# The first batch of an attention and SwiGLU kernel: its loads in one GpSimd queue, its values among its scores, and tile 0's down projection by halves

## The chip, the cores and the metric

One core of a Trainium2 chip runs the whole kernel. The metric is the device time of one execution in microseconds (us); lower is better.

## What is computed

Selective attention over 8 batches of 8 heads (576 positions, head width 64), and a SwiGLU block on its output (4608 tokens, width 512, hidden width 1536):

```python
scores = 0.125 * q @ k.T                       # per batch and head, 576 x 576
cum = cumsum(maximum(s, 0))
scores = where(causal, -1e9, scores + minimum(-(cum[i] - cum[j]), 0))
attn = exp(scores - max); attn = attn / sum(attn)
x = (attn @ v), heads side by side             # 4608 x 512
out = (silu(x @ w_gate) * (x @ w_val)) @ w_out
```

Inputs and output are float32; the kernel multiplies in bfloat16.

## The kernel before, in words

**Heads and half batches.** The 64 heads are counted through (`bh`), eight per batch; four of them are a half batch (`hb`, 0 to 15). k and q of a half batch are loaded as float32 (`load_one`), cast to bfloat16 (`cast_one`), transposed, and laid into one of two sets of buffers `KQ` (`hb % 2`), two heads to a row (`r`). Half batches 0 to 4 are transposed by TensorE (`pe_transpose`) and copied out of PSUM (`pe_out`: k by ScalarE, q by VectorE); half batches from 5 on go through a scratch in DRAM (`scratch`, buffers `ks`, `qs`) and a DMA transpose (`transposes`, into `pk`, `pq`), and VectorE lays them into `KQ` (`split`). The bias of s is carried by extra rows of `KQ` that small DMAs fill from `HL` (`aug`).

**Scores and values.** `score_piece` multiplies one of four pieces of a head's causal scores (four diagonal blocks; 448 + 64; 320 + 192; 64 columns), and ScalarE takes the exponential (L388) into `pt`. GpSimd then zeroes the upper triangles of the diagonal blocks (L391, L396). In batch 0 the pieces go by pairs into two wide PSUM buffers of 1024 columns, so that there are two exponentials a head; later heads have one bank and one exponential for each piece. `av_piece` multiplies with v (`VT`, cast by `cast_v`, L183), `av_out` divides by the row sum (L429, L430), and x is transposed for the block by TensorE (`x_pe`, batches 0 and 1) or through DRAM (`x_out`, `x_in`).

**The SwiGLU block** works on nine tiles of 512 tokens. For each of 12 column groups `ft`: gate product (L626), tanh on ScalarE (`th`, L631), `pp` on VectorE (L633), value product (L641), `ht` on VectorE (L649). Then the down projection: tiles 0 and 1 by `down_plain` (L670), the rest by a seven product scheme (`down_seven`, L711).

**Order.** Each engine's instructions run in the order in which the code writes them. Batch 0 is written out by hand in `first_batch`: all scores, then all values and x. From then on the generator `ffn_items` yields an item after each product, and after item n the loop pumps the attention of later heads (`attn_items`) to a position that grows evenly with n; in tile 0 this starts after item 6. `hook[n]` holds extra work for item n of tile 0, `PREP_AT` the pieces after which TensorE transposes a coming half batch, `side` the loads, casts and scratch work at given pieces, and `later` the `split` copies, of which one is issued at every fourth item and the rest ahead of the next half batch:

```python
if step == 0:
    do_later(NR * 2)
...
for ci in range(4):
    score_piece(kk, ci)
    side(h, step, ci)
```

**Queues.** k, q and v are loaded by DMAs that SP issues, in the order of the code; the weights, which are cast on the way, and stores are issued by GpSimd. Early in batch 0, SP issues s, k and q of half batches 0 and 1, the bias rows, v of batch 0 and k, q of half batch 2; at head 7 it issues k, q 3, v of batch 1, k, q 4 and 5. GpSimd issues gate and value weights at heads 1, 4 and 5, and `wo` at head 7.

**PSUM.** `take` gives out the bank that was released the longest ago, `give` returns it; after batch 0 the two wide buffers and four single ones are replaced by eight single banks.

Of the kernel before, what the change touches and what calls it, by code (L numbers as in the profile page):

```python
# [12 lines left out]
FP32 = mybir.dt.float32  # L13
# [6 lines left out]
def kernel(  # L20
# [86 lines left out]
    PTP = {0: first, "bufs": 8}  # L107

    with tc.manual_schedule():
# [3 lines left out]
        first_psum = ExitStack()  # L113
        psa = first_psum.enter_context(tc.tile_pool(name="psa", bufs=1, space=PSUM))
        bank = {}
        for i in range(2):
            bank["w", i] = psa.tile([128, 1024], FP32, name=f"wide{i}")
        for i in range(4):
            bank["s", i] = psa.tile([128, 512], FP32, name=f"one{i}")
        released = {key: i - 8 for i, key in enumerate(bank)}  # L120
# [3 lines left out]
        def take(kind="s"):  # L124
            b = min((x for x in bank if x[0] == kind), key=lambda x: released[x])
            assert released[b] < OPEN
            released[b] = OPEN
            return b
# [5 lines left out]
        def second_psum():  # L134
            assert all(x < OPEN for x in released.values())
            at_end = dict(released)
            first_psum.close()
            psb = ctx.enter_context(tc.tile_pool(name="psb", bufs=1, space=PSUM))
            bank.clear()
            released.clear()  # L140
            for i in range(8):
                bank["s", i] = psb.tile([128, 512], FP32, name=f"bank{i}")
                released["s", i] = at_end["w", i // 2] if i < 4 else at_end["s", i - 4]

# [6 lines left out]
        def load_one(hb, name, rs=(0, NR)):  # L151
# [3 lines left out]
            nc.sync.dma_start(  # L155
# [10 lines left out]
        def load_v(b, cs):  # L166
# [3 lines left out]
            for c in cs:  # L170
                n = 128 if c < 4 else TAIL
                nc.sync.dma_start(
# [13 lines left out]
        NEGS2 = -1.0058441162109375  # L186

# [22 lines left out]
        load_qk(1)  # L210
# [6 lines left out]
        make_identity(nc, ident)  # L217

# [10 lines left out]
        pads(0)  # L229
        init_vt(0)  # L230
        init_vt(1)
        nc.vector.memset(aug_rows(1, 0), 0.0)
        nc.gpsimd.memset(aug_rows(1, 1), 0.0)
        pads(1)
# [113 lines left out]
        scs = {}  # L348

        def score_piece(bh, ci):  # L350
            hb, hh = divmod(bh, HB)
            pair = bh < H
            if ci == 0:
                pts[bh] = PTP[0].tile(
                [128, PTW], BF16, tag="pt", bufs=PTP["bufs"], name="pt"
            )
# [3 lines left out]
            if pair:  # L360
                if ci % 2 == 0:
                    bs = take("w")
                    scs[bh] = bs
                else:
                    bs = scs[bh]
                base = (512, 0, 0, 512)[ci]
            else:
                bs = take()
                base = 0
            o = base  # L370
            n = sum(hi - lo for _, lo, hi in CHUNKS[ci])
            sc = view(bs, 1024 if pair else 512)
            for (tj, lo, hi) in CHUNKS[ci]:
# [5 lines left out]
                    start=True,  # L379
                    stop=True,  # L380
                )
                o += w
            if not pair or ci % 2 == 1:
                if pair:
                    c0, W = ((576, 1024), (0, 576))[ci // 2]
                else:
                    c0, W = CHUNK_PT[ci], n
                nc.scalar.activation(pt[:, c0 : c0 + W], sc[:, 0:W], AF.Exp, scale=0.125)  # L388
                give(bs)
            if ci == (1 if pair else 0):  # L390
# [90 lines left out]
        def side(h, step, ci):  # L481
            bh = HB * h + step
            if bh == H + 3 and ci == 1:
                for c in range(5):
                    cast_v(1, c, nc.gpsimd)
            if h >= 3 and h + 3 < NHB and (step, ci) == (0, 1):
                load_qk(h + 3)
            hb = h + 1
            if NPE <= hb < NHB:
                late = hb == NPE  # L490
                if (step, ci) == (0, 1):
# [515 lines left out]
```

The softmax here doesn't subtract the row's maximum and nothing guards it: scores larger than these inputs give would overflow.

## Time and profile before

| | |
|---|---|
| Median of 9 runs | 379.78 us (378.94 to 381.06) |
| The profiled execution's own time | 379.78 us |
| Its span in the profile | 378.0 us |
| TensorE busy (matmuls) | 362.9 us |
| VectorE busy | 290.4 us |
| ScalarE busy | 242.6 us |
| GpSimd busy | 207.1 us |
| First matmul at | 5.40 us |
| First gate product at | 31.56 us |

The profile shows one execution. PE is TensorE, PEld its loading of weights, DVE is VectorE, ACT ScalarE, POOL GpSimd and SP SyncE, which only issues DMAs here. A busy TensorE is not one at its peak: four matmuls of 512 columns in a row show 379 ns each, but follow each other every 0.86 us by four. What counts for the end is when TensorE stands still. The span leaves out about 1.8 us around the program that the time contains.

### The profile page before, as it was taken

To read this page: it belongs to the slowest core of one execution; us is meant where nothing else is said; L and a number is where in the kernel's file an instruction comes from. 1 tells how busy PE (TensorE), PEld (TensorE's weight loads), DVE (VectorE), ACT (ScalarE), POOL (GpSimd) and SP (SyncE) were. 2 spreads that over 40 slices of the span, in tenths; PEclk is the share of its full clock that TensorE was granted. 3 is DMA by queue.
4 is the path that set the end of the run, shared out by engine and by line. 5 is a ranking of instruction groups with operands and counts; after the bars stand their busy time and mean duration, and the time that the engine had idled before them with its cause. 6 is when DMAs were issued, how large, how long until landed. Compare 5 with 4: busy or idle time off the path is not lost.

```text
span 378.0 us, 8674 instructions
## 1 busy us (share of the span) xinstructions
PE 362.9 (96%) x3246; PEld 230.3 (61%) x3246; DVE 290.4 (77%) x577; ACT 242.6 (64%) x459; POOL 207.1 (55%) x326
## 2 busy tenths in 40 slices
PE   3879999999999999999999999999999999999996
PEld 3666556655555545865586558655875575466465
DVE  8766787457894899769975998589958876985984
ACT  7686788677976877578766885697365523323321
POOL 7684348545374646595559556875675426224320
PEclk9999999999999999999999999999999999999999
DMA  7999999997477998499769765986223133001103
GB/s 250 186 252 263 198 249 278 343 269 162 166 181 241 220 294 212 111 249 249 197 186 285 199 161 164 237 207 144 51 73 111 25 27 128 0 2 69 42 2 111
DMA packets 100729, 64.22 MB, mean 170 GB/s; under 512 B 81888, under 2 KB 85824, under 8 KB 100688
## 3 DMA queue, kind: packets, MB, share of 16 engines
q1 hardware_dynamic: 91248, 46.15, 49.2%
q0 software_dynamic: 9440, 17.53, 18.4%
q8 instruction: 25, 0.41, 0.4%
q14 instruction: 16, 0.13, 0.1%
HBM read 37.90 MB, written 19.86 MB: 153 GB/s over the span
## 4 chain that ended last, share of the span: by engine, by line
PE 87%; DVE 4%; DMA 3%; ACT 3%; issue 1%; SPq 0%; DVEq 0%; ACTq 0%
PE bank L626 22%; PE bank L641 22%; PE bank L711 17%; PE bank L375 9%; PE bank L413 7%; PE bank L670 5%; DMA pk<-ks 2%; PE wide L375 2%; DVE pp L633 1%; ACT pt L388 1%; DVE kq L326 1%; DMA rawq<-in_q_dram 1%; DVE ht L649 1%; PE one L413 1%; PE one L311 1%
## 5 line engine op out<-in xcount | busy, mean ns | idle before, releaser
L388 ACT ACTIVATE pt<-bank 128x512 bf16<-128x512 f32 x224 | 106.8, 506 | 25.8 <-PE bank L375 17.0
L626 PE MATMUL bank<-XT,wg 128*128 128x512 bf16 x432 | 110.8, 379 | 0.8 <-DVE ht L649 0.3
L641 PE MATMUL bank<-XT,wv 128*128 128x512 bf16 x432 | 110.9, 379 | 0.0
L631 ACT ACTIVATE th<-bank 128x512 bf16<-128x512 f32 x108 | 64.7, 599 | 58.9 <-PE bank L626 54.6
L633 DVE SCALAR_TENSOR_TENSOR pp<-th,bank 128x512 bf16<-128x512 bf16 x108 | 73.7, 683 | 24.3 <-ACT th L631 23.7
L649 DVE SCALAR_TENSOR_TENSOR ht<-pp,bank 128x512 bf16<-128x512 bf16 x108 | 74.1, 687 | 10.4
L658 POOL TENSOR_TENSOR ht<-ht 128x512 bf16<-128x512 bf16 x35 | 40.4, 1155 | 53.0 <-DVE su L656 52.9
L375 PE MATMUL bank<-kq 128*128 128x128 bf16 (+4 forms) x504 | 67.5, 240 | 0.2 <-DVE ht L649 0.2
L375 PEld LDWEIGHTS <-kq 128*128 128x128 bf16 x576 | 47.0, 100 | 32.7 <-issue 5.3
L626 PEld LDWEIGHTS <-wg 128*128 128x128 bf16 x432 | 38.4, 98 | 35.2 <-issue 1.2
L641 PEld LDWEIGHTS <-wv 128*128 128x128 bf16 x432 | 38.3, 98 | 35.3
L391 POOL TENSOR_SCALAR_AFFINE_SELECT pt<-pt 128x512 bf16<-128x512 bf16 x64 | 41.8, 653 | 30.0 <-ACT pt L388 29.3
L413 PEld LDWEIGHTS <-pt 128*128 128x128 bf16 x960 | 41.0, 98 | 16.6 <-issue 0.8
L413 PE MATMUL bank<-vt,pt 128*128 128x65 bf16 x840 | 41.8, 194 | 0.5 <-DVE ot L430 0.5
L447 POOL DMA_DIRECT2D xs<-ot x24 | 21.7, 906 | 28.1 <-DVE ot L430 28.1
L711 PEld LDWEIGHTS <-ht 128*128 128x128 bf16 x336 | 31.2, 98 | 4.3
L197 POOL DMA_DIRECT2D kq<-HL x52 | 32.1, 619 | 0.1
L430 DVE TENSOR_TENSOR ot<-bank,rc 128x320 bf16<-128x320 f32 x56 | 27.5, 491 | 1.9
L396 POOL TENSOR_SCALAR_AFFINE_SELECT pt<-pt 128x64 bf16<-128x64 bf16 x64 | 17.3, 270 | 18.5 <-ACT pt L388 18.4
L711 PEld LDWEIGHTS <-su 128*128 128x128 bf16 x252 | 23.6, 98 | 3.3
L670 PE MATMUL bank<-wo,ht 128*128 128x512 bf16 x96 | 24.6, 379 | 0.0
L776 POOL TENSOR_TENSOR ysb<-ysb 128x512 f32<-128x512 f32 x12 | 15.2, 1270 | 15.3 <-DVE ysb L770 15.3
(96 smaller groups left out, 397.7 us busy)
## 6 DMA issues: line engine op xcount, KB each, us to landing
rawk<-in_k_dram SPq DMA_DIRECT2D x15, 576.0 KB
rawq<-in_q_dram SPq DMA_DIRECT2D x15, 576.0 KB
rawv<-in_v_dram SPq DMA_DIRECT2D x32, 256.0 KB
out_dram<-ysb POOLq DMA_DIRECT2D x32, 256.0 KB, 3.7
xs<-ot POOLq DMA_DIRECT2D x24, 160.0 KB, 3.7
ks<-ck SPq DMA_DIRECT2D x11, 288.0 KB
qs<-cq SPq DMA_DIRECT2D x11, 288.0 KB
wg<-in_moe_w_gate_dram POOLq DMA_DIRECT2D x2, 768.0 KB, 12.9
```

Of the source, the lines that this page charges most:

```text
L375: nc.tensor.matmul(sc[:, o : o + w], T[:, 1, e * S + 128 * tj : e * S + 128 * (tj + 1)], T[:, 0, e * S + lo : e * S + hi], start=True, sto ...
L388: nc.scalar.activation(pt[:, c0 : c0 + W], sc[:, 0:W], AF.Exp, scale=0.125)
L391: nc.gpsimd.affine_select(pt[:, 1088:1600], pt[:, 1088:1600], pattern=[[0, 4], [1, 128]], compare_op=ALU.is_ge, fill=zreg, base=0, channel ...
L413: nc.tensor.matmul(av[:, bi * (D + 1) : (bi + 1) * (D + 1)], pt[:, c0 : c0 + 128], VT[b % 2][:, tj, h, :], start=(tj == 0), stop=(tj == bi),)
L626: nc.tensor.matmul(pg, WG[j][:, c, f0 : f0 + 128], xt[:, c, :], start=(c == 0), stop=(c == 3),)
L631: nc.scalar.activation(th, pg, AF.Tanh, scale=0.5)
L633: nc.vector.scalar_tensor_tensor(pp, in0=th, scalar=1.0, in1=pg, op0=ALU.add, op1=ALU.mult)
L641: nc.tensor.matmul(pv, WV[j][:, c, f0 : f0 + 128], xt[:, c, :], start=(c == 0), stop=(c == 3),)
L649: nc.vector.scalar_tensor_tensor(hp[:, 2 * k2 : 2 * k2 + 2, :].rearrange("p a n -> p (a n)"), in0=pp, scalar=0.5, in1=pv, op0=ALU.mult, op ...
L658: (nc.vector if ft == NFT - 1 else nc.gpsimd).tensor_sub(hp[:, 1:3, :], hp[:, 1:4:2, :], hp[:, 0:3:2, :])
L670: nc.tensor.matmul(py, hps[ft // 2][:, 2 * (ft % 2) + half, c0 : c0 + 128], WO[ft // WKO][:, ft % WKO, :], start=(ft == 0), stop=(ft == NF ...
L711: nc.tensor.matmul(ps, lhs(p), rhs(p), start=(first and p == 0), stop=(last and p == NP - 1), skip_group_check=True,)
```

## The change

In batch 0 the wide buffers go; every piece of scores has a bank and an exponential of its own, and the causal mask is added by a matmul (`ident` with `lower`, a tile of 0 and -32768) instead of GpSimd's selects. Values and the transposes of x are written between the scores of later heads, from head 4 on. Of each of the first three column groups, three of the four gate products of tile 0 are written ahead of the last x (`products`, which keeps a begun bank). k, q 1, v 0, the weights of gate and value (now in halves), k, q 2 to 5, v 1 and v 2 are loaded through GpSimd's queue, in the order in which they are used; all of v 0 is cast on GpSimd. `hook` spreads the later loads over tile 0. k, q 3 are transposed later, and k, q 5 are cast and go through the scratch later. In `prep_one` the second copy out of PSUM is put off to the next item (`seconds`). In tile 0 the down projection does the first half of the hidden width for all four groups of 128 tokens, then the second half, with four banks open.

```diff
-    PTP = {0: first, "bufs": 8}
+    PTP = {0: first, "bufs": 7}
+    lower = first.tile([128, 512], BF16)
...
-            bank["w", i] = psa.tile([128, 1024], FP32, name=f"wide{i}")
...
+        bank = {i: psb.tile([128, 512], FP32, name=f"bank{i}") for i in range(8)}
...
+        nc.gpsimd.memset(lower, 0.0)
+        nc.gpsimd.affine_select(
+            lower, lower, pattern=[[0, 4], [1, 128]],
+            compare_op=ALU.is_ge, fill=nc.gpsimd.to_reg(MASKED), base=0, channel_multiplier=-1,
+        )
...
+        for nm in ("k", "q"):
+            load_one(1, nm, eng=nc.gpsimd)
         init_vt(0)
...
+            masked_here = masked and ci in (0, 3)
+            if masked_here:
+                nc.tensor.matmul(
+                    sc, ident, lower[:, 0:n], start=True, stop=False, skip_group_check=True
+                )
...
+            nc.scalar.activation(pt[:, c0 : c0 + n], sc, AF.Exp, scale=0.125)
+            give(bs)
+            if masked:
+                return
...
         def side(h, step, ci):
             bh = HB * h + step
-            if bh == H + 3 and ci == 1:
+            if bh == H + 4 and ci == 1:
                 for c in range(5):
                     cast_v(1, c, nc.gpsimd)
+            if h == 4 and (step, ci) in ((0, 1), (2, 1)):
+                load_qk(6 + step // 2)
...
+                if late and (step, ci) == (0, 0):
+                    cast_one(hb, "k", nc.scalar)
+                if late and (step, ci) == (0, 2):
+                    cast_one(hb, "q", nc.scalar)
+                if late and (step, ci) == (1, 0):
+                    scratch(hb)
+                if late and (step, ci) == (1, 1):
+                    transposes(hb)
...
-                first = 1 if hb < NPE + 2 else 0
+                first = 2 if late else 1 if hb < NPE + 3 else 0
...
         def prep_one(hb, i):
...
-            for r in range(2):
-                pe_out(hb, nm, g, r, nc.scalar if nm == "k" else nc.vector)
+            eng = nc.scalar if nm == "k" else nc.vector
+            pe_out(hb, nm, g, 0, eng)
+            seconds.append(lambda: pe_out(hb, nm, g, 1, eng))
         PREP_AT = {
-            2: {(0, 3): 0, (1, 3): 1, (2, 1): 2, (2, 3): 3},
+            2: {(2, 0): 0, (2, 2): 1, (3, 0): 2, (3, 2): 3},
...
+        def products(kind, ft, xt, cs=range(4)):
+            j, f0 = divmod(ft * 128, WCH)
+            w = (WG if kind == "g" else WV)[j]
+            if (kind, ft) in begun:
+                bs, c0 = begun.pop((kind, ft))
+                cs = range(c0, 4)
+            else:
+                bs = take()
+            for c in cs:
+                nc.tensor.matmul(
+                    view(bs, TT), w[:, c, f0 : f0 + 128], xt[:, c, :],
+                    start=(c == 0), stop=(c == 3),
+                )
+            if cs[-1] < 3:
+                begun[kind, ft] = bs, cs[-1] + 1
+            return bs
...
         def down_plain(tt, hps):
...
+            order = [(ts_, j) for ts_ in range(4) for j in range(NWCH)]
+            if tt == 0:
+                order.sort(key=lambda x: x[1])
+            for ts_, j in order:
+                yield from part(ts_, j)
...
+        keep_warm(32)
         cast_half(0, "k", 0, nc.scalar)
         cast_half(0, "q", 0, nc.scalar)
         aug(0, SP4)
+        row_half("k", 0, nc.scalar)
+        row_half("q", 0, nc.vector)
+        cast_half(0, "k", 1, nc.scalar)
+        cast_half(0, "q", 1, nc.gpsimd)
+        load_v(0, (0, 1), nc.gpsimd)
+        nc.gpsimd.memset(aug_rows(1, 1), 0.0)
+        pads(1)
+        aug(1, SP4)
+        load_v(0, (2, 3, 4), nc.gpsimd)
+        w_load("g", 0)
+        keep_warm(10)
+        row_half("k", 1, nc.scalar)
+        row_half("q", 1, nc.vector)
+        keep_warm(10)
+        cast_one(1, "k", nc.vector)
+        cast_one(1, "q", nc.vector)
+        for c in range(3):
+            cast_v(0, c, nc.gpsimd)
+        w_load("v", 0, 0)
+        for c in range(3, 5):
+            cast_v(0, c, nc.gpsimd)
+        for nm in ("k", "q"):
+            load_one(2, nm, eng=nc.gpsimd)
+        w_load("v", 0, 1)
+        for nm in ("g", "v"):
+            w_load(nm, 1, 0)
+        for nm in ("k", "q"):
+            load_one(3, nm, eng=nc.gpsimd)
+        for nm in ("g", "v"):
+            w_load(nm, 1, 1)
+        scores(0)
+        half_batch("k")
+        scores(1)
+        half_batch("q")
+        scores(2)
+        scores(3)
...
+        load_v(1, range(5), nc.gpsimd)
+        scores(4)
+        values(0, 1)
+        scores(5)
+        values(2, 3)
+        scores(6)
+        values(4)
+        x_pe(0, nc.vector)
+        scores(7)
+        aug(3, SP4)
+        values(5)
+        x_pe(1, nc.vector)
+        values(6)
+        x_pe(2, nc.scalar)
+        values(7)
+        for ft in range(3):
+            products("g", ft, XT[:, :, 0:TT], range(3))
+            if ft == 0:
+                x_pe(3, nc.scalar)
...
+        for i in range(4):
+            at_item(3 + i, prep_one, 2, i)
+        at_item(8, load_one, 4, "k", (0, NR), nc.gpsimd)
+        at_item(10, cast_one, 3, "k", nc.gpsimd)
+        at_item(11, w_load, "o", 0)
+        at_item(13, w_load, "o", 1)
...
-            n0 = 6 if tt == 0 else 0
+            n0 = 7 if tt == 0 else 0
```

`row_half` transposes and copies one row of half batch 0, `half_batch` transposes k or q of half batch 1 and copies its first row, `scores(h)` is four times `score_piece`, `values` is `av_piece` and `av_out`, and `keep_warm(n)` multiplies `ident` with itself n times into a spare bank.

## The prediction

> **What bounds the kernel now.** I read the page's busy times first:
>
> ```profile
> span 378.0 us, 8674 instructions
> PE 362.9 (96%) x3246; PEld 230.3 (61%) x3246; DVE 290.4 (77%) x577; ACT 242.6 (64%) x459; POOL 207.1 (55%) x326
> ```
>
> TensorE is idle for 378.0 - 362.9 = 15.1 us. By the busy time per stretch: 5.4 before its first instruction, 4.4 between 5.4 and 25, 0.36 in 30 to 35, 0.5 in 40 to 50, 0.74 in 120 to 150, 3.7 at the end. All else is a gapless TensorE stream, so only idle time that goes or comes matters. The change works in the first 90 us; there the chain of waits, in order of time (start, length, what), shows what held TensorE:
>
> ```profile
> 18.50 1.03 ACT pt L388
> 19.54 0.04 issue
> 19.58 0.62 PE wide L375 x6
> 20.20 0.02 issue
> 20.22 1.03 ACT pt L388
> ...
> 23.01 0.95 PE wide L375 x9
> 23.96 0.92 PE one L413 x30
> ...
> 30.87 0.65 ACT XT L468
> 31.52 0.04 issue
> 31.56 1.04 PE bank L626 x4
> ```
>
> One head of batch 0 takes 20.22 - 18.50 = 1.72 us: ScalarE empties the wide buffer (1.03), TensorE refills it (0.62), neither overlaps the other. All values (L413) come after the scores; the dense stream (L626) starts at 31.56. Two rows on DMA (columns: stretch; busy us of PE, PEld, DVE, ACT, POOL; clock; DMA share; GB/s) show the queues nearly empty, because the loads of v stand behind other work on SP until 10.89:
>
> ```profile
> 10.00:11.00 1.00, 0.96 (x8) 0.62 (x7) 1.00 (x2) 0.31 (x1) 1.00 (x3) 1.00 0.29 77
> 11.00:12.00 1.00, 0.86 (x5) 0.51 (x4) 0.97 (x2) 0.58 (x1) 0.54 (x1) 1.00 0.14 25
> ```
>
> [...]18 early transposes took 2.13 us, 118 ns each; four at 65.76 took 0.22, 55 each[...]. [...] from 13 to 46 us the DMA share stays over 1.0 while SP and POOL both issue. [...] here the `xs` stores took 2.7 at least, 3.7 at the median.
>
> **The change, part by part.** Median and profiled execution are both 379.78 (span 378.0 plus 1.8 around it), so sums against one stand against the other.
>
> *Start of the scores.* 32 warming matmuls fill the wait for the first load: free, TensorE is idle until 5.40. Ten more before the scores cost 10 x 56 ns = 0.6; the warm clock saves about as much on 18 transposes (2.13 to about 1.0). The mask of `lower` and its select put about 1.1 us ahead on POOL, and its loads of k, q 1 start near 4.4 instead of 3.5; POOL waits for q's second half until 8.33 anyway. On SP only s, k, q 0 and the bias rows (`aug`) are left, so nothing stands ahead of these; all loads up to batch 2's v go to POOL. First scores stay at 10.35 (±0.5).
>
> *Scores of batch 0.* Four exponentials per head (three of 512, one of 64) instead of two. A later row has four of L388 in 1.69 us, so about 1.6 a head against 1.72. The mask's matmuls (8 x 216 ns, 8 x 30 ns: 2.0 us in all) replace 16 POOL selects; half lie under ScalarE, half on the path later: a head is then 0.93 on TensorE (0.22 + 0.22 + 0.25 of L375 in the chain, 0.25 of mask). Five heads from 10.95, plus 0.45 for the cast of k 1 on DVE (until 11.9): TensorE has issued head 4 and stands at `values(0, 1)` at 18.7.
>
> *Arrival of v, the first new wait.* v is now issued by POOL instead of SP, and its last two chunks are cast by POOL instead of VectorE, one instruction after another. Rows for the prices (mean ns):
>
> ```profile
> L447 POOL DMA_DIRECT2D xs<-ot x24 | 21.7, 906 | 28.1 <-DVE ot L430 28.1
> L683 POOL DMA_DIRECT2D out_dram<-ysb x8 | 4.6, 575 | 0.0
> L183 POOL CAST vt<-rawv 128x512 bf16<-128x512 f32 (+1 forms) x13 | 7.7, 615 | 3.5 <-DMA rawv<-in_v_dram 3.4
> ```
>
> 640 runs cost 906, 128 runs 575: 0.65 ns a run; a chunk of v (1024 runs) is estimated at 1.17 us, the tail (512) at 0.82. From POOL's cast of q (ends 8.99): two chunks 2.34, memset 1.10, pads 0.43, two chunks 2.34, tail 0.82, gate weights 0.78, three casts 1.73, value weights 0.77, two casts 1.17, gaps 0.4: **20.9**. TensorE stands 2.2 us, with scores 5 to 7 queued behind it, and ScalarE starves. Bounds: 0.5 us (a chunk at 0.9, TensorE late) to 3.5 (each landing late[...]).
>
> *To the first gate products.* From 20.9 on TensorE's own order: the last value of head 0 0.04, value heads 1 to 7 7 x 0.56, scores 3 x 0.93, three x transposes 3 x 0.36: 7.83, giving 28.7. Two of the four copies into `XT` go from ScalarE (0.64) to VectorE (0.45), beside this. Three products 0.65, wait for `ot` of head 7 until 29.5, transposes 0.36, six products 1.29: at 31.2 nine products (1.94) are done. Before, none was done at 31.56. **Lead 2.3 us.**
>
> *Tile 0's first items.* Since 1.94 us of matmul is done early, VectorE sets the pace, though each second q copy is put off by one item. Its work from the first `pp` (31.2 + 0.22 + 0.7 = 32.1) to the last copy that head 8 needs: three pp/ht pairs 4.1, three q copies 2.4: 38.6. TensorE is there at 37.15 and stands 1.5 us (0.5 to 2). Compared at the end of the sixth gate product (42.2, against 44.42 less 0.72 of scores and transposes not yet done in the changed order, 43.7): **lead 1.5**; the difference is what VectorE took back.
>
> *k, q of heads 12 to 15.* `PREP_AT` moves the last transposes to two pieces before head 12: value product, four transposes, one 64-column piece, then head 12. VectorE must do `ht` (0.69) and a q copy (0.7) after that product, while TensorE has 0.25 us left: **a stall of 1.1** (0.5 to 1.6). Before, none lay there.
>
> *k, q of heads 20 to 23.* Casts on ScalarE (1.15 each, between exponentials) now start at head 16 instead of in heads 12 to 15 (59.6 and 64.4 before). Before, the copy came ahead of head 20:
>
> ```profile
> 87.25 0.57 DVE L284 COPY kq<-pq 64x1152 bf16<-64x1152 bf16 x1
> ...
> 88.75 0.39 PE L375 MATMUL bank<-kq 128*128 128x128 bf16 x4
> ```
>
> In the new order three of the four copies stand between a `pp` and head 20: after the gate product tanh 0.65, pp 0.7, two copies 0.9 = 2.3, TensorE has 1.4 of work: **0.9** (0 to 3; the upper end if `pq` lands late: scratch near 77.5, its landing 2 to 6, transposes 4 to 9 in this trace).
>
> *At nothing.* Weights: by the rates of this trace (340 GB/s plain, 230 for v, about 170 for the casting loads) POOL's queue lands the first gate weights near 22.5 and the second halves near 43; use is at 29 and 51. If POOL is throttled by its semaphores, the casts of k 3 (due 45.8, ready about 44) go first. Selects of heads 8 on wait behind loads until about 42; values use them at 53. Casts of v 1 end about when used. Down projection by halves: the same matmuls; it covers a late second half of `wo`, which wasn't late before (no wait at L670). Its four open banks leave four for scores: 0.3 for one bank reused after 0.9 us of TensorE work. Finer yields cost nothing: the matmuls are the same.
>
> **Sum**: -1.5 + 1.1 + 0.9 + 0.3 = +0.8; 379.8 + 0.8 = **380.6**.
>
> **Rivals.** *The lead survives* (ends faster): v lands and is cast by the time TensorE gets there (wait 0.5 instead of 2.2, lead 3.2 after VectorE's part) and VectorE is ahead at heads 12 and 20 (0.3 each). 379.8 - 3.2 + 0.6 + 0.3 = 377.5, down to 376.5 without those stalls. For it: 4.4 us of idle time to take. Against: POOL's sum. It decides once v is ready before about 19.5. *The scratch chain becomes the bound*: `pq` lands 2 us late, VectorE stands and TensorE behind it, as in 120 to 150: 382.6. *It doesn't do what it says*: POOL's order is ruled by its semaphore waits, the weights come as before, and start and tile 0 cancel: 379.8.
>
> **Chances**: given back 0.45 (own range 379.7 to 381.6), survives 0.30, scratch chain or a later v 0.15, no change 0.10. A measurement can tell about 0.2% (0.76 us) from no change. Slower: 0.34 of the first and 0.15 = 0.49; same: 0.11 of the first, 0.09 of the last = 0.20; faster 0.31. Leaving a tenth out on each side, the range is 377.0 to 382.6.
>
> **What would show it.** TensorE waiting for POOL's `vt` near 19 to 21 (right) or not at all; first gate product near 28.8; a wait for DVE `kq` ahead of heads 8, 12 and 20 of 1.5, 1.1 and 0.9; no wait for DMA of weights. A gapless stream from 29 us on would make me wrong toward 377; an idle TensorE of several us on a weight or `pq` would make me wrong upward.

## The result, and the profile after

The changed kernel takes 382.99 us (median of 17 runs, 381.8 to 387.4), the kernel before beside it 380.12 (54 runs): the ratio is 1.0079, 95% interval 1.0065 to 1.0093. By that ratio it is 3.0 us slower (2.9 by the medians); forecast was 0.8. The profiled execution of the changed kernel took 383.99, 1.0 above its median; its span, 382.3, is compared with the 378.0 of before.

Its busy times stand first on the page:

```profile
span 382.3 us, 8804 instructions
PE 366.3 (96%) x3300; PEld 231.4 (61%) x3300; DVE 290.0 (76%) x577; ACT 242.0 (63%) x473; POOL 221.8 (58%) x338
```

TensorE's 366.3 is no measure of gain: the warming matmuls of the first 5 us (3.59) are in it, and so are matmuls at half clock (3.41 us from 53.0 on, below). Its line of time tells more. The chain of waits after (start, length, what), for the start:

```profile
7.72 4.59 DMA kq<-HL
...
12.35 0.83 PE bank L358 x8
...
19.05 0.38 PE bank L352
19.43 0.71 PE bank L358 x8
...
20.20 0.92 PE bank L395 x30
...
29.59 2.69 PE bank L627 x12
```

The bias rows (`kq<-HL`) land at 12.31, so the first scores (L358) start at 12.35 and not at 10.34. The values (L395) then follow at 20.20 without a wait for v, and the dense stream is reached at 29.59, 1.97 before the 31.56 of the kernel before. The new start is a gain even so. It is lost later; these are the stands of TensorE (times at which it waits) after the start, from its timeline (start, length, ..., in brackets the idle time and what ended it):

```profile
38.32 0.82 PE L358 MATMUL bank<-kq 128*128 128x128 bf16 x8 [1.35 <-DVE kq L315]
52.85 0.47 PE L358 MATMUL bank<-kq 128*128 128x128 bf16 x4 [1.97 <-DVE kq L315]
91.56 0.40 PE L358 MATMUL bank<-kq 128*128 128x128 bf16 x4 [1.04 <-DVE kq L273]
305.16 0.36 PE L395 MATMUL bank<-vt,pt 128*128 128x65 bf16 x6 [0.87 <-DVE ht L654]
```

The first three are heads 8, 12 and 20, each waiting for the last copy of its k and q. The fourth is in the last third, where the change moves nothing. At head 12 the kernel before has no stand; in its chain of waits the end of head 11 and the beginning of head 12 (L375) lie without a gap between two products:

```profile
51.04 0.86 PE bank L626 x4
51.91 0.47 PE bank L375 x7
52.38 0.86 PE bank L641 x4
```

Behind the second stand of the changed kernel lies one more loss. Two rows by the microsecond (stretch; busy us of PE, PEld, DVE, ACT, POOL; clock; DMA share; GB/s):

```profile
51.00:52.00 1.00, 0.00 (x0) 0.00 (x0) 0.90 (x2) 0.97 (x2) 0.38 (x1) 1.00 1.16 265
...
53.00:54.00 1.00, 1.00 (x7) 0.44 (x5) 0.00 (x0) 0.60 (x1) 0.00 (x0) 0.50 1.19 278
```

The granted clock is 0.50 for 3.41 us from 53.0 on; eight matmuls of 512 columns take 3.33 in the chain there, 1.73 elsewhere. By an estimate from these numbers, half of the 3.41 us, 1.7, is the most that is lost there. Not every execution has it: a fall of this length lowers the mean clock of the span by 0.0045, and 10 of 18 executions, the profiled one among them, have a mean below 0.997. Their median is 383.82, that of the other eight 382.16. The mean doesn't say where a fall lies; only the profiles do. The clock also falls after TensorE's last product (at 380.69 in the changed kernel, 2.5 after it), but in the sixteen profiles this lowers the mean by 0.0025 at most and costs nothing. And falls are not peculiar to the new order: of 131 executions of the kernel before that were timed beside the experiments, 16 have a mean below 0.997, at no cost that shows (median 379.77, of the others 379.89).

To see where time comes and goes I compare points that lie at the same place of the work in both kernels: starts of exponentials (four for each head) and of tanh (`th`, one for each gate product, 108 in all). Negative is ahead of the kernel before, us; the other columns are experiments told below. Only tanh 1 is no such point, since the changed order has other work behind it there.

| start of | before at | changed | e2_prep | e8_three | e14_early3 | e13_before_late |
|---|---|---|---|---|---|---|
| tanh 1 | 32.67 | -1.42 | -1.67 | -1.24 | -2.01 | -0.41 |
| head 14 | 63.39 | +1.40 | -0.90 | -0.48 | -1.66 | +1.64 |
| head 24 | 107.03 | +2.82 | +0.53 | +0.38 | -0.74 | +1.64 |
| tanh 82 | 300.24 | +2.82 | +0.50 | +1.13 | -0.19 | +1.42 |
| tanh 85 | 315.45 | +3.87 | +1.55 | +1.13 | -0.19 | +1.42 |
| end of span | 377.95 | +4.33 | +1.89 | +1.30 | 0.00 | +1.42 |

At head 14 the changed kernel is 1.40 behind. The stand at head 12 is 1.97 of that. The fall of the clock is about 1.1: the profile of e7_xs_sp, the same program up to there, had no fall and stood at -0.29, after a start that was 0.55 sooner. e6_splits, the same program up to there too, gives the like: it reaches head 12 within 0.03 us of e7_xs_sp, has the fall, and is 1.10 behind it at head 14. Without the two the changed kernel would be 1.7 ahead. From there it loses 1.42 up to head 24 (1.04 of it the stand at head 20), 1.05 between tanh 82 and 85, and 0.46 at the end.

### The profile page after: what moved, and what is told of

Same layout as the page of the kernel before. It is cut to its first block, busy times and chain, and to the rows that moved or that the text cites. A ratio compares the mean times of both kernels' runs of the same rounds, so it can differ in the third digit from the quotient of the medians.

```text
span 382.3 us, 8804 instructions
## 1 busy us (share of the span) xinstructions
PE 366.3 (96%) x3300; PEld 231.4 (61%) x3300; DVE 290.0 (76%) x577; ACT 242.0 (63%) x473; POOL 221.8 (58%) x338
## 4 chain that ended last, share of the span: by engine, by line
PE 84%; DVE 9%; ACT 2%; DMA 2%; issue 1%; DVEq 0%; ACTq 0%; SPq 0%
PE bank L627 44%; PE bank L726 15%; PE bank L358 10%; PE bank L395 7%; PE bank L677 5%; DVE ht L654 2%; DVE pp L643 2%; ACT pt L368 1%; DVE kq L273 1%; DMA kq<-HL 1%; DVE ot L412 1%; PE bank L445 1%; PE bank L286 1%; DMA s_sb<-in_s_dram 1%; DVE kq L315 1%
## 5 line engine op out<-in xcount | busy, mean ns | idle before, releaser
L368 ACT ACTIVATE pt<-bank 128x512 bf16<-128x512 f32 (+1 forms) x256 | 121.0, 511 | 34.8 <-PE bank L358 21.9
L358 PE MATMUL bank<-kq 128*128 128x128 bf16 (+4 forms) x576 | 75.1, 240 | 5.7 <-DVE kq L315 3.3
L358 PEld LDWEIGHTS <-kq 128*128 128x128 bf16 x576 | 45.6, 98 | 35.9 <-issue 5.5
L373 POOL TENSOR_SCALAR_AFFINE_SELECT pt<-pt 128x512 bf16<-128x512 bf16 x56 | 36.8, 657 | 27.7 <-ACT pt L368 26.7
L395 PEld LDWEIGHTS <-pt 128*128 128x128 bf16 x960 | 41.5, 98 | 18.6 <-POOL pt L373 1.0
L395 PE MATMUL bank<-vt,pt 128*128 128x65 bf16 x960 | 46.8, 194 | 1.4 <-DVE ht L654 0.9
L412 DVE TENSOR_TENSOR ot<-bank,rc 128x320 bf16<-128x320 f32 x64 | 31.5, 492 | 2.2
L183 POOL DMA_DIRECT2D kq<-HL x48 | 28.9, 604 | 0.8 <-issue 0.7
L677 PE MATMUL bank<-wo,ht 128*128 128x512 bf16 x96 | 25.9, 379 | 0.0
L411 DVE RECIPROCAL rc<-bank 128x5 f32<-128x5 f32 x64 | 12.1, 188 | 15.2 <-PE bank L395 14.6
```

Source lines behind the costliest of these rows:

```text
L358: nc.tensor.matmul(sc[:, o : o + w], T[:, 1, e * S + 128 * tj : e * S + 128 * (tj + 1)], T[:, 0, e * S + lo : e * S + hi], start=not maske ...
L368: nc.scalar.activation(pt[:, c0 : c0 + n], sc, AF.Exp, scale=0.125)
L373: nc.gpsimd.affine_select(pt[:, 1088:1600], pt[:, 1088:1600], pattern=[[0, 4], [1, 128]], compare_op=ALU.is_ge, fill=zreg, base=0, channel ...
L395: nc.tensor.matmul(av[:, bi * (D + 1) : (bi + 1) * (D + 1)], pt[:, c0 : c0 + 128], VT[b % 2][:, tj, h, :], start=(tj == 0), stop=(tj == bi),)
L412: nc.vector.tensor_mul(ot[:, :, e * D : (e + 1) * D], av3[:, :, 0:D], rc[:, :, None].to_broadcast([128, NCH, D]),)
L677: nc.tensor.matmul(view(pys[ts_], DM), hps[ft // 2][:, 2 * (ft % 2) + half, c0 : c0 + 128], WO[j][:, ft % WKO, :], start=(ft == 0), stop=( ...
```

## The experiments

Each was timed in turn with the kernel before; "before" is the median of that kernel in the same set of runs. `+` and `-` are against the changed kernel unless said otherwise. "Full clock" are the executions with a mean clock of 0.997 or more, a "fallen" clock is a mean below that, wherever in the span the fall lies.

### The start

**e1_kq1_sp**: k, q 1 back in SP's queue.

```diff
             load_one(0, "q", (r, r + 1))
+        load_qk(1)
...
-        for nm in ("k", "q"):
-            load_one(1, nm, eng=nc.gpsimd)
```

> The changed kernel with the loads of k 1 and q 1 back on SP, right behind those of q 0, as in the kernel before; everything else of the change stays. Theory A (the bias rows of `aug(0)` took 4.59 us instead of about 2.4 because two GpSimd loads ran beside them): the rows land near 10.3 and the first scores start near 10.4 instead of 12.35; TensorE then meets v, whose casts ended at 19.43, some 1.5 us sooner, so of the 2.0 us between 0.5 and 2.0 remain and the time falls to 381.0 to 382.5. Theory B (the rows are late because of what SP or VectorE do ahead of them): the first scores stay at 12.3 and the time at 383.0 or above. Theory C (the added mask and warm-up products are the loss): the start moves, the end does not: 383.0.

385.16 (before 379.83): slower than the changed kernel, ratio to before 1.0139 (1.0107 to 1.0171). The first scores do start earlier, at 11.04, but the time goes to the next thing in the queue, k 1. The chain of waits:

```profile
3.01 5.77 DMA rawq<-in_q_dram
...
11.64 1.74 DVE ck L244
...
13.43 0.68 PE bank L285 x9
```

The cast of k 1 ends at 13.38 and the transposes (L285) stand 1.50 for it; the stream of gate products starts no sooner (29.80). So moving k, q 1 to GpSimd is worth its place, and undoing it is no remedy. None of the theories foresaw the slowdown itself. In this profile 1.77 of it is a stand at 148.5 us, behind one VectorE add of `su` that took 2.62 us, where the median of these adds is 0.29. Whether every execution has it is not shown.

**e9_swap**, run later, on top of three edits told below: the first loads of v go behind GpSimd's memsets.

```diff
-        load_v(0, (0, 1), nc.gpsimd)
         nc.gpsimd.memset(aug_rows(1, 1), 0.0)
         pads(1)
+        load_v(0, (0, 1), nc.gpsimd)
         aug(1, SP4)
```

> The three edits, and at the start the two loads of v (0, 1) behind GpSimd's memsets for half-batch 1 instead of ahead of them, so that they are issued near 10.6 instead of 8.6; the last load of v keeps its time. Theory A (the rows of `aug(0)` are late because k 1, q 1 and, from 8.6 on, v keep the DMA engines without a gap): the first rows land near 10.5, the first scores start at 10.5 to 11.0, and the time is 0.5 to 1.5 below that of the three edits alone: 378.5 to 379.5. Theory B (the rows are late for k 1 and q 1 alone, or by chance): the scores start at 11.5 to 12.5 as before and the time is the same as of the three edits, or higher, as v may then come late at 20.

380.24 (before 379.99; ratio 1.0005, 0.9992 to 1.0018), against 380.55 for the three edits alone: 0.3, which the intervals don't tell apart. The first scores, one profile for each kernel: 10.77, and 11.06, 10.95 and 11.77 in the three kernels built on this one, mean 11.14. With the order of the changed kernel, eight profiles have 10.55 to 13.46, mean 11.87; with the kernel before's start, three have 10.34, 11.23 and 11.46. The direction is that of theory A; the ranges overlap, and the gain in time is below the 0.5 that it named. It also shows that 10.34, on which the forecast rested, was an early execution. And with an early start the forecast's wait for v appears, small: TensorE waits 0.33 for POOL's `vt` at 19.2.

### Head 12

**e2_prep**: k, q 3 are prepared earlier.

```diff
-            2: {(2, 0): 0, (2, 2): 1, (3, 0): 2, (3, 2): 3},
+            2: {(1, 3): 0, (2, 1): 1, (2, 3): 2, (3, 1): 3},
```

> The changed kernel with the preparation of k and q 3 spread over (1,3), (2,1), (2,3), (3,1) of heads 9 to 11 instead of (2,0), (2,2), (3,0), (3,2). Theory A (head 12 stands 2.0 us behind the last copy on VectorE, and the clock falls to half after that stand in some executions): no stand of over 0.6 us ahead of head 12, no slice at half clock, time lower by 1.5 to 3.0 us: 380.0 to 381.5. Theory B (VectorE is full in tile 0, the stand comes back in another place): the stand moves to head 10 or 11, or to gate products, with 1.5 us or more, and the time stays within 0.5 of 383.0. A third way: the casts of k and q 3 on GpSimd end too late for the earlier place, and TensorE stands at the transposes near 44 for 1 us: 382.0.

381.69 (before 379.83; ratio 1.0053, 1.0032 to 1.0073). TensorE's timeline has 0.89 where it had 1.97, and five of six executions keep the full clock:

```profile
51.68 0.38 PE L358 MATMUL bank<-kq 128*128 128x128 bf16 x4 [0.89 <-DVE kq L315]
```

The stand shrinks by half rather than to under 0.6, the time goes down by 1.3, less than theory A named. No stand of 1.5 came elsewhere, so B falls.

**e13_before_late**: the kernel before, with this one part of the change alone.

```diff
-            2: {(0, 3): 0, (1, 3): 1, (2, 1): 2, (2, 3): 3},
+            2: {(2, 0): 0, (2, 2): 1, (3, 0): 2, (3, 2): 3},
```

> The kernel before with one part of the change alone: k and q 3 prepared at (2,0), (2,2), (3,0), (3,2) instead of (0,3), (1,3), (2,1), (2,3). Theory A (the later preparation by itself makes head 12 stand behind VectorE): a stand of 1.0 to 2.2 us ahead of head 12, in some executions a fall of the clock behind it, and 381.0 to 382.0, 1.0 to 2.0 above the kernel before. Theory B (the stand needs the new start, the deferred second copies or the order of the loads with it): below 0.5 us at head 12 and within 0.4 of the kernel before.

382.93 (before 379.89; ratio 1.0070, 1.0053 to 1.0088). By itself the later preparation costs 3.0 us, as much as the whole change, and more than theory A named. TensorE's timeline:

```profile
53.70 0.38 PE L375 MATMUL bank<-kq 128*128 128x128 bf16 x4 [2.52 <-DVE kq L326]
```

The chain of waits there goes from the gate product over an exponential, tanh (0.60) and `pp` (0.69) to the first of two copies (0.63); VectorE itself waits 0.97 for tanh, so this stand is not VectorE's row alone. 16 of 22 executions have a fallen clock, median 383.33; the six at full clock, the profiled one among them, have 380.89. So an execution that keeps the clock loses about 1.0 (1.42 in the profile). The 2.4 between the two groups is more than the 1.7 that one fall can take, and no fallen execution was profiled; what else these lose is not shown.

**e15_late_fill**: the same kernel, with work of no use in the stand.

```diff
+                    if kk == 12:
+                        fb = take()
+                        for _ in range(32):
+                            nc.tensor.matmul(view(fb, 128), ident, ident, start=True, stop=True)
+                        give(fb)
```

> The kernel before with the late preparation of k and q 3, as in e13_before_late (382.93), and 32 matmuls of 128 columns of no use to the result ahead of head 12. Theory A (the stand of 2.5 us lets the clock fall to half, which costs 1.2 in most executions): TensorE stands idle for 1.0 us or less there, the clock stays at full in most executions and the time is 381.2 to 382.0. Theory B (the clock has nothing to do with it, the time is lost by the stand and what it delays): 382.7 to 383.5.

381.60 (before 379.84; ratio 1.0044, 1.0030 to 1.0058): 1.3 us less than without the 32 matmuls, though head 12 starts no sooner. Only 4 of 21 executions have a fallen clock. (At full clock the 17 are at 381.37, above the six at 380.89 without the matmuls, so the gain comes from fewer falls.)

```profile
51.20 1.95 PE L560 MATMUL bank<-ident 128*128 128x128 bf16 x32
53.87 0.38 PE L375 MATMUL bank<-kq 128*128 128x128 bf16 x4 [0.72 <-DVE kq L326]
```

4 of 21 is also about what the kernel before has in the same set (6 of 34). That is theory A: with work in the stand, the falls went from 16 of 22 executions to 4 of 21. Of the 3.0 us, 1.3 go with it; the other 1.7 stay, since head 12 still waits.

The clock on record shows more. In each of the sixteen traces its changes lie on a grid of 3.413 us, whose position differs from execution to execution (in the changed kernel 5.22, 53.01, 56.42 and 380.69 us: 14, 1 and 95 steps). In these five the stand was followed by a fall where 1.97 us of TensorE's idle time lay in one step of the grid, and by none where the step held 1.58 or less:

| profile | stand at head 12 | steps of the grid that hold it | idle in each | clock in the next step |
|---|---|---|---|---|
| changed kernel | 1.97 | 49.59 to 53.01 | 1.97 | 0.50 |
| e6_splits | 1.97 | 49.86 to 53.28 | 1.97 | 0.50 |
| e7_xs_sp | 1.97 | 48.49 to 51.90, to 55.31 | 1.58, 0.39 | 1.00 |
| e12_down | 1.98 | 48.37 to 51.78, to 55.19 | 0.82, 1.17 | 1.00 |
| e13_before_late | 2.52 | 48.93 to 52.34, to 55.75 | 1.17, 1.35 | 1.00 |

The stand of e13_before_late was the longest of the five, and its profile kept the clock: a border of the grid cut the stand in two, 1.17 and 1.35.

**e5_fill12** had tried the same in the changed kernel, with 24 matmuls ahead of head 12:

> The changed kernel with 24 matmuls of 128 columns into a free bank ahead of head 12, of no use to the result, so that TensorE does not stand idle while it waits for the last copy of k and q 3. Nothing else moves. Theory A (the clock falls to half because of the 2 us stand, and costs 1.2 to 1.8 us in the executions where it falls): TensorE stands idle for less than 0.8 us ahead of head 12, the clock stays at 1.0 from 52 to 58, head 12 starts no later than in the changed kernel; the time is lower by 0.3 to 1.5 and the profile has 50 to 60 at full clock. Theory B (the fall of the clock at 53 to 57 has nothing to do with the stand): the clock falls all the same, the time stays at 383.0 or rises by up to 0.7 us for the 24 matmuls.

382.46 (before 379.83; ratio 1.0083, 1.0053 to 1.0112). Five of six executions keep the full clock, as theory A has it, and their median, 382.17, is that of the changed kernel's executions at full clock (382.16). The ratio over all six is that of the changed kernel: six runs could not show a gain.

### Head 20, and the stand at 304

**e3_head20**: the chain of half-batch 5 one head earlier.

```diff
+            if hb == NPE and (step, ci) == (3, 0):     # hb = h + 2
+                cast_one(hb, "k", nc.scalar)
+            if hb == NPE and (step, ci) == (3, 2):
+                cast_one(hb, "q", nc.scalar)
...
-                first = 2 if late else 1 if hb < NPE + 3 else 0
+                first = 1 if hb < NPE + 3 else 0
```

(The scratch goes from (1, 0) to (0, 0), the transposes from (1, 1) to (0, 1).)

> The changed kernel with the chain of half-batch 5 one head earlier: casts at head 15 instead of 16, scratch and transposes at head 16 instead of 17, splits on VectorE at heads 17 and 18. Theory A (head 20 stands 1.0 us for the last split): the stand is gone or below 0.2, the time falls by 0.8 to 1.2 us: 382.0. Theory B (VectorE sets the pace there, so that a wait only moves): a wait of about the same length for ht or kq at heads 17 to 19, the time stays within 0.3 of 383.0. A third way: the casts come too soon for the loads of k and q 5 and hold ScalarE: slower by 0.5 or more.

387.68 (before 379.83; ratio 1.0190, 1.0161 to 1.0218): the worst of all, by a way that no theory named. All six executions are above the slowest but one of the changed kernel (384.02). The chain of the profiled execution, the slowest of the six at 391.55:

```profile
77.36 8.02 DMA pk<-ks
...
86.31 0.77 DVE kq L273
...
87.11 0.47 DVE XT L452
...
87.62 1.44 PE bank L627 x3
```

The transpose takes 8.02 us from issue to landing. A copy out of `pk` was put on VectorE before that landing and waited 4.5 us for it; the copy into `XT` queued behind it, which the gate products need, started only when the copies out of `pk` were done, at 87.11. TensorE stands 3.62 us and the clock is at half for the 6.83 us from 86.45 on. (This execution has two falls more, at 14.77 and 55.73, which the edit doesn't touch, so its own time is no measure of the edit.) In the changed kernel, with `first = 2`, the transpose is issued only 1.6 later (78.97), but the first copy out of `pk` runs at 88.96 and shows no wait for it. That the stand of 1.0 at head 20 is the smaller price of this is likely, not shown.

**e6_splits**: two of those four copies on ScalarE.

```diff
-            nc.vector.tensor_copy(
+            (nc.scalar.copy if (hb, name) == (NPE, "q") else nc.vector.tensor_copy)(
```

> The changed kernel with the two copies of q of half-batch 5 (`split`, 0.46 us each on VectorE) on ScalarE; the two of k stay on VectorE. Theory A (head 20 stands 1.04 us because VectorE has pp, ht, rc, ot and four copies in one unbroken row from 81 to 91): the stand falls to 0.3 or less, the time by 0.7 to 1.1 us: 382.0. Theory B (the transposes' landing or ScalarE's casts set head 20): the stand stays at 0.8 or more, or ScalarE's longer row makes th late; 383.0 or above.

383.08 (before 379.99; ratio 1.0101, 1.0062 to 1.0139). In the profile the stand goes from 1.04 to 0.48, and 0.85 is lost from head 14 to 24 instead of 1.42. The median shows nothing of it: five of these six executions have a fallen clock, the profiled one at head 12, which this edit leaves alone. By time it is inconclusive.

**e7_xs_sp**: the last two stores of attention rows by SP.

```diff
-            nc.gpsimd.dma_start(
+            (nc.sync if pr >= 14 else nc.gpsimd).dma_start(
```

> The changed kernel with the last two stores of attention rows (`xs`, pairs 14 and 15) issued by SP instead of GpSimd. Theory A (TensorE stands 0.87 us at 304 because GpSimd began the issue of the last but one 1.85 us after its data were ready, and the mask select of the next head stood behind it): the stand of 0.87 is gone, the items from 84 on are 0.9 sooner against the kernel before, and the time falls by 0.8 to 1.0: 382.0. Theory B (the stand is a bank's or VectorE's, and GpSimd only looks late): the stand stays, the time is 383.0 within 0.3.

The reason to try it are three lines of GpSimd's timeline, the first of the kernel before, then two of the changed kernel:

```profile
298.07 0.89 POOL L447 DMA_DIRECT2D xs<-ot  x1 [2.50 <-DVE ot L430]
```

```profile
302.45 0.89 POOL L429 DMA_DIRECT2D xs<-ot  x1 [4.06 <-DVE pp L643]
...
304.46 0.64 POOL L373 TENSOR_SCALAR_AFFINE_SELECT pt<-pt 128x512 bf16<-128x512 bf16 x1
```

Before, the issue starts 0.29 after `ot` is done; in the changed kernel 1.85 after it, and the mask select behind it ends at 305.1, when TensorE goes on. With the store on SP the stand at 304 is gone from the profile, and so is the +1.05 between tanh 82 and 85. By time 382.76 (before 379.99; ratio 1.0073, 1.0050 to 1.0097) tells nothing, again with five of six executions at fallen clock. So GpSimd's late issue is shown as the cause of this stand; the name `ht` in the list of waits was the instruction that ended at about the same moment. Why the issue came late, in an order of instructions that is the same there as before, is not. It begins just as a `pp` of VectorE ends (302.45); whether that is more than chance, no run tests.

### The order of the down projection

**e12_down**: tile 0's down projection in the old order.

```diff
-            if tt == 0:
-                order.sort(key=lambda x: x[1])
```

> The changed kernel with the down projection of tile 0 in the order of before (row block by row block, over the whole width) and the rest of the change as it is. The prediction put the new order at nothing: then the time stays at 383.0 within 0.4 and no wait for `wo` is seen. If the halves of the width were of use (the second half of WO, whose load is now issued at item 13, lands after the old order needs it), TensorE waits at L677 for a load of `wo` by 0.5 us or more, and the time rises to 383.5 or above. If the halves are what costs (four banks open at once), it falls by 0.3 or more.

382.49 (before 379.89; ratio 1.0061, 1.0046 to 1.0076), and 382.30 at full clock against 382.16 for the changed kernel. No wait for `wo` appears. The median alone is 0.5 lower, which the expectation would read as a cost of the halves; but two of these six executions have a fallen clock against ten of the changed kernel's eighteen, and at full clock the difference is gone. So the halves cost nothing and bring nothing here that six runs can show.

### Put together

**e8_three**: e2_prep, e6_splits and e7_xs_sp in one kernel.

> The changed kernel with three of these edits together: k and q 3 prepared over heads 9 to 11 from (1,3) on, the copies of q of half-batch 5 on ScalarE, the last two stores of rows by SP. Theory A (the loss is the sum of single stands after the first batch, each with its own cause): stands of 2.0, 1.0 and 0.9 with the fall of the clock go, 1.0 us or so remains at head 12, and the time is 379.3 to 380.3, the kernel before within 0.5 us. Theory B (each stand that goes comes back in another place, because VectorE or GpSimd is full): 381.5 or above.

380.55 (22 runs; before 379.99; ratio 1.0019, 1.0007 to 1.0031): 2.4 us under the changed kernel, just above the band of theory A and clear of B's. The stands are separate; of their lengths, 1.1 at head 12, 0.56 at head 20 and all of the 0.87 at 304 can be taken away. **e10_act2** adds, to e9_swap, q's first copies of half-batch 2 on ScalarE, **e11_act23** those of half-batch 3 too:

```diff
-            pe_out(hb, nm, g, 0, eng)
+            pe_out(hb, nm, g, 0, nc.scalar if hb == 2 else eng)     # e11: nc.scalar
```

> The version with three edits and the swapped loads of v, and the first copies of q of half-batch 2 (0.7 to 0.8 us each, two of them) on ScalarE instead of VectorE. Theory A (head 8 stands 1.35 us because VectorE has pp, ht and these copies in one row from 30.9 to 37.3, while ScalarE is free in between): the stand ahead of head 8 falls to 0.5 or less, the time is 379.3 to 379.7, under the kernel before by up to 0.6. Theory B (ScalarE's row of th and six copies is then the longer one, so that th and with it the gate products come late): the stand stays over 1.0 or moves to a gate product; 380.2 or above.

> As the last, with the first copies of q of half-batch 3 on ScalarE too. Theory A (what is left of the stand at head 12, 0.88 us, is VectorE's row as well): it falls to 0.3 or less, and the time to 378.5 to 379.2, faster than both kernels. Theory B (ScalarE has the exponentials of heads 9 to 11 and th there, so that the copies come no sooner): the stand at head 12 stays at 0.8 or more, the time is that of the last kernel or up to 0.5 higher.

379.98 and 380.16 (before 379.89; ratios 1.0003, 0.9993 to 1.0014, and 1.0004, 0.9990 to 1.0017). Head 8's stand falls from 1.35 to 0.76 in both, head 12's only to 0.78 in the second. For head 12 theory B is right; for head 8 neither is, as the stand halves without falling to the 0.5 that theory A named. In the first a new wait of 1.55 appears at the transposes, for the cast of k 3 on GpSimd.

**e14_early3** moves the loads and casts of k, q 3 forward as well, and prepares them where the kernel before did:

```diff
+        for nm in ("k", "q"):
+            load_one(3, nm, eng=nc.gpsimd)
         w_load("v", 0, 1)
         for nm in ("g", "v"):
             w_load(nm, 1, 0)
-        for nm in ("k", "q"):
-            load_one(3, nm, eng=nc.gpsimd)
...
-        at_item(10, cast_one, 3, "k", nc.gpsimd)
-        at_item(11, cast_one, 3, "q", nc.gpsimd)
+        at_item(7, cast_one, 3, "k", nc.gpsimd)
+        at_item(8, cast_one, 3, "q", nc.gpsimd)
```

> The last combined version with the loads of k and q 3 ahead of the value weights of the first width and the weights of the second in GpSimd's queue, their casts at items 7 and 8 instead of 10 and 11, and their preparation at (0,3), (1,3), (2,1), (2,3) as in the kernel before. Theory A (the stand of 0.8 at head 12 is left over from the late casts, and the lead of the start is lost there): the stand falls below 0.3, the time to 378.6 to 379.4, faster than both kernels by up to 1.2. Theory B (the lead is lost in any case, since VectorE and GpSimd have no room in tile 0: the stands come back at heads 9 to 11, at the transposes, or as a wait for value weights): 379.9 or above.

379.99 (before 379.84; ratio 1.0009, 0.9994 to 1.0025). The stand at head 12 is gone and the kernel is 1.66 ahead at head 14; at the end of the span nothing is left. 0.92 go up to head 24: 0.48 is the stand that remains at head 20, and about 0.4 without a stand is lost there in every version with the new order (1.42 with a stand of 1.04 in the changed kernel), while e13_before_late loses nothing. Another 0.55 go in small steps up to tanh 82. Neither is settled. So theory A is right on the stand and wrong on the time. No version is faster than the kernel before by more than the measurement can tell.

## Why the prediction was wrong, step by step

The sign of the likeliest case was right, the size was not: +0.8 forecast, +3.0 measured, just above the range. The step that failed is the term for head 12: it priced the stand at 1.1, where it was 1.97, and left out the fall of the clock behind it.

- **Start of the scores, 10.35**: 12.35 in this execution, and on average about 0.9 later than with the old start (11.87 in eight profiles, 11.01 in three). "On SP only s, k, q 0 and the bias rows are left, so nothing stands ahead of these" looked at the issuing queue alone. The rows were issued at 7.72, no later than the 7.93 of the kernel before, and took 4.59 while the DMA engines were still moving k, q 1 and then v: their share was 1.07, 0.75, 0.84 and 0.91 in the four microseconds from 8 to 12, at 248 to 359 GB/s, where the kernel before has 1.03, 0.76, 0.29 and 0.14. That these transfers hold the rows back is what e9_swap speaks for, without proving it. With the warming matmuls ahead of them, the 18 transposes right before the first scores took 1.20 us (8.90 to 10.10), where they had taken 2.13. (The forecast's reading that the DMA share stays over 1.0 from 13 to 46 us misses one microsecond, 18 to 19, with 0.98; nothing rests on that.)
- **Arrival of v, 20.9, a wait of 2.2**: the last cast ended at 19.43 and there was no wait. The issue of a chunk of v took 0.9 (two in 1.79), not the estimated 1.17, and all of v 4.5 instead of 5.5; and TensorE came to `values(0, 1)` at 20.2 instead of 18.7. Two errors of opposite sign met: gate products at 29.59 against 28.7.
- **Tile 0's first items, lead 1.5**: right in size. The sixth gate product ended at about 41.8, where the forecast had 42.2. Seen from head 14, with the stand and the fall taken out, the lead was 1.7; VectorE set the pace, and head 8 stood 1.35 against 1.5.
- **Head 12, +1.1**: this is the step that failed. The wait itself, for VectorE's last copy, was the one that was forecast; its size was not. The stand was 1.97 here and 2.52 with this part alone. The forecast let VectorE do `ht` and one copy after the last value product. In the changed kernel the chain of waits has one copy more in front, put off from the item before, so that `pp`, too, comes late:

```profile
49.84 0.83 DVE kq L315
...
50.70 0.70 DVE pp L643
...
51.49 0.69 DVE ht L654
52.17 0.63 DVE kq L315
```

  Another term was left out altogether: the fall of the clock, 1.1 in the profiles and by the estimate at most 1.7, in 10 of 18 executions. Moved alone, the later preparation makes e13_before_late 3.0 slower, where the sum had 1.1.
- **Head 20, +0.9**: a stand of 1.04. Right, and for the reason given, VectorE's row of `pp`, `ht` and copies (with two of the copies on ScalarE it was 0.48); 0.4 more goes there without a stand.
- **At nothing**: the weights brought no wait of more than 0.3, and the down projection in halves was free (e12_down); the 0.3 for a reused bank was not found. The stand of 0.87 at 304 was in no term, nor could it be read from the change, and 0.46 at the end isn't traced.

With the measured terms (the lead is what is left when stand and fall are taken off) the profiled execution has -1.7 (lead) + 2.0 (head 12) + 1.1 (clock) + 1.4 (head 14 to 24) + 1.05 + 0.46 = +4.3 in its span, where the forecast had -1.5 + 1.1 + 0 + 0.9 + 0.3 + 0. The executions at full clock are 382.16 - 380.12 = 2.0 slower; the half with a fall brings the median to 3.0.

Of the rivals, *the lead survives* had the right condition (v ready before 19.5, and it was, at 19.43) and still the wrong end: the time saved at the start has to pass VectorE and head 12. *The scratch chain becomes the bound* is what e3_head20 made of the kernel, not the change.

## What to carry to other kernels

Before you count a lead at the start as time, follow it to the first place where the engine that gets the work is in step with another: here VectorE paces tile 0 and holds the copies for head 12, and a lead of 1.7 us was spent there. A step that is moved later onto an engine without room must be priced with everything in front of it on that engine, and a stand like the one of 1.97 us on TensorE also with a fall of the clock, which took 1.1 us more here. One profile does not show whether a kernel has such falls: compare the mean clocks of many executions. When several stands are suspected, take the moved parts singly into the kernel before: one such run put as much as the whole loss on one part, where three edits of the changed kernel only bounded it.

## What the runs showed of the hardware that was not expected

- **The clock fell after 1.97 us or more of idle time in one step of its grid.** The steps are of 3.413 us. In the sixteen traces 1738 steps at full clock can be read. All 22 with 1.97 us or more without a matmul (six in the stream, sixteen at the end) were followed by half clock; of the others, which have 1.92 at most, one was (e8_three, 1.58 from 4.79 on). The falls in the stream lasted one step (3.41 us), in e3_head20 once two (6.83). If the grid lies by chance, a stand of 1.97 brings a fall in about 0.4 of the executions and one of 2.52 in about 0.6 (estimates from these lengths, the step of 3.413 and 1.97 as the limit). Measured, falls elsewhere included, were 10 of 18 and 16 of 22; with stands of about 0.9 it was 1 of 6 (e2_prep) and 3 of 22 (e8_three, whose one profiled fall lay at 8.21, not at head 12), no clear excess over the 16 of 131 of the kernel before.
- **The bias rows took longer, and varied more, with the changed order of loads.** They (four transfers of 9 KB) took 3.64 to 5.90 us from issue to landing in six profiles with that order, against 3.25 and 3.48 in two with the old one, and at most 2.4 for the first of them in the kernel before (issued at 7.93, the first scores right behind them at 10.34). The first scores, with the same start of the program, came anywhere from 10.55 to 13.46 us. That the large transfers under way beside them are the reason is likely, not shown.
- **GpSimd's issue of one DMA started late.** That of an `xs` store (at 302.45) began 1.85 us after its data in the changed kernel, 0.29 in the kernel before, with the same order of instructions. The cause is open.
